# An FNet and SoLU kernel: block moves in runs of 256 bytes on two queues, one store for both batches, and a turn in five parts

## The chip, the cores and the metric

The kernel runs on one core of a Trainium2 chip. The metric is the device time of one execution in microseconds (us). Ratios are the mean time of one kernel's fast runs over that of the other's from the same rounds on the same chip, so they are not quite the ratio of the medians that stand beside them. The intervals are 95% intervals.

## The reference

```python
def _attn_ref(x):                        # x: 8 x 3136 x 256
    X = np.fft.fft(x, axis=1)
    X = np.fft.fft(X, axis=2)
    return X.real.astype(np.float32)

def _moe_ref(x, w_in, w_out, g_ln):      # x: the above as 25088 x 256, d_ff = 1024
    h = x @ w_in
    h_max = np.max(h, axis=-1, keepdims=True)
    e = np.exp(h - h_max)
    sm = e / (np.sum(e, axis=-1, keepdims=True) + 1e-09)
    solu = h * sm
    mu = np.mean(solu, axis=-1, keepdims=True)
    var = np.mean((solu - mu) ** 2, axis=-1, keepdims=True)
    ln = (solu - mu) / np.sqrt(var + 1e-06) * g_ln
    return (ln @ w_out).astype(np.float32)
```

## The kernel before

The batches go in four pairs. The sequence transform of 3136 = 49 x 64 is done in two steps; a pair has 25 values of k1, and each (pair, k1) is a *unit* of work: up-projection `ps_h` (line L195), SoLU on VectorE and ScalarE, down-projection `ps_o` (L276), store. There are 100 units. Three things matter here.

First, the activations must be transposed between the two projections. VectorE transposes blocks of 32 x 32 into `v`, and 16 DMAs of 64 KB, "moves", carry blocks between partitions into `uT`, which is the stationary operand of the down-projection.

```python
    def turn_blocks(t, s):
        if s == 0:
            t.v = fpool.tile([P, 4, 32, KF, 2], FP32, tag="v", name="v32", bufs=2)
        u = t.u[s].rearrange("p (c q r) -> p c q r", q=4, r=32)
        for o in (s,) if len(t.signs) == 2 else (0, 1):
            nc.vector.transpose(out=t.v[:, :, :, :, o].rearrange("p q n c -> p c q n"), in_=u)

    def move_blocks(t):
        t.uT = fpool.tile([P, 4, 32, KF, 2], FP32, tag="uT", name="uT", bufs=3)
        for i in range(4):
            for q in range(4):
                a, b = slice(32 * i, 32 * i + 32), slice(32 * q, 32 * q + 32)
                nc.sync.dma_start(out=t.uT[b, i], in_=t.v[a, q])

    def down(t, s):
        uT = t.uT.rearrange("p i n c s -> p (i n) c s")
        # ... 8 matmuls: nc.tensor.matmul(ps, uT[:, :, c, s], Wo[:, c, :], ...)
```

The last two indices of `v` and `uT` are c (8) and s (2): a run is 32 x 8 x 2 floats = 2 KB, and neighbouring n lie 64 bytes apart. Second, the results of a unit are stored by two DMAs, one a batch, and the mirrored ones by an indirect DMA. Third, `turn` brings a pair's sequence transform back from HBM with the roles of its indices exchanged: 3.2 MB on the sync queue, just before the pair is needed.

The main loop of units, in which every engine's program has this order:

```python
        for i in range(len(units) + 2):            # cur = unit i, nxt = i + 1, old = i - 2
            even(cur, up(cur, 0)); odd = up(cur, 1)
            nxt.q = take2(transform2(pairs[nxt.p], nxt.k1))
            join(cur, odd); expo(cur)
            ahead_pe(ahd, cur.k1)                  # the next pair's transform, and its turn
            ps_o = [down(old, s) for s in old.signs]
            for s in cur.signs: product(cur, s)
            for s in cur.signs: square(cur, s); turn_blocks(cur, s)
            store(old, 0, ps_o[0])
            move_blocks(cur); stats(cur)
            # ... loads of the next pair
            store(old, 1, ps_o[1])
```

(The conditions at the ends of the loop are cut.)

## Time and profile before

| | before |
|---|---|
| median of 3 runs | 1442.1 us (1441.77 to 1443.86) |
| TensorE busy | 1239.2 us, 86% |
| VectorE busy | 1084.9 us, 75% |
| DMA share, all queues of part 3 added | 51% |
| TensorE waits for `uT` | 79.5 us |

A profile page reads as follows: a group's line has the busy time and mean duration of one instruction, and after the second bar the time its engine sat idle just before, with what ended it. The chain of waits follows the last instruction back to what released it. TensorE's records overlap, so the mean duration of one is no pace (its busy time counts an overlap once); paces are taken from the timeline. The lines that carry the argument stand in the prediction.

### The profile page before, as it was taken

How to read it: one execution, taken by the hardware profiler on the slowest of the kernel's cores; microseconds unless marked ns; L12 is line 12 of the kernel's file. 1: busy time of each engine (PE TensorE's matmuls, PEld its weight loads, DVE VectorE, ACT ScalarE, POOL GpSimd, SP SyncE). 2: the span in 40 equal slices, each digit the busy share in tenths (PEclk: the TensorE clock that was granted, in tenths of full speed). 3: DMA queues.
4: the chain of work that ended last, by engine and by line, in shares of the span. 5: the costliest groups of instructions: out<-in, count | busy, mean ns of one | idle time of the engine just before them, and what ended most of it. 6: DMA issues, size and time to landing. Idle time of an engine off the chain costs nothing.

```text
span 1438.1 us, 17170 instructions
## 1 busy us (share of the span) xinstructions
PE 1239.2 (86%) x4864; PEld 996.2 (69%) x4864; DVE 1084.9 (75%) x1481; ACT 611.9 (43%) x1149; POOL 482.8 (34%) x892
## 2 busy tenths in 40 slices
PE   1543799999959999989959999999978999999996
PEld 1312587777848778878848778777857777878876
DVE  2597888787866688887857688877857778888881
ACT  1100445454434355544534444545524445444442
POOL 3400344443312345434213344434313223333331
PEclk8666899999989999999989999999998999999998
DMA  9540455554474555555474545555474444444443
GB/s 251 185 84 0 125 149 148 146 152 130 127 163 109 142 137 154 150 154 131 122 164 111 149 125 158 144 148 137 120 171 112 114 104 113 112 110 114 114 113 82
DMA packets 128318, 189.66 MB, mean 132 GB/s; under 512 B 36726, under 2 KB 63102, under 8 KB 127968
## 3 DMA queue, kind: packets, MB, share of 16 engines
q1 hardware_dynamic: 113552, 157.61, 43.6%
q0 software_dynamic: 8704, 25.44, 5.7%
q10 hardware_dynamic: 5968, 5.52, 1.7%
q8 instruction: 40, 0.66, 0.2%
q14 instruction: 54, 0.44, 0.1%
HBM read 44.78 MB, written 38.80 MB: 58 GB/s over the span
## 4 chain that ended last, share of the span: by engine, by line
PE 53%; SPq 24%; DMA 9%; DVE 8%; issue 4%; ACT 1%; POOL 1%; POOLq 0%; DVEq 0%; ACTq 0%
PE ps_o L276 33%; SPq L270 21%; PE ps_h L195 15%; DMA g<-zd 3%; DMA uT<-v 3%; PE ps L149 2%; SPq L290 2%; PE ps L169 2%; DMA xa<-in_x_dram 2%; DVE ex L303 2%; DVE h L209 1%; DVE v L262 1%; DMA xb<-in_x_dram,idx 1%; DVE y L111 1%; DMA out_dram<-ot 1%
## 5 line engine op out<-in xcount | busy, mean ns | idle before, releaser
L276 PE MATMUL ps_o<-Wo,uT 128*128 128x256 f32 x3136 | 750.3, 399 | 92.8 <-DMA uT<-v 79.5
L276 PEld LDWEIGHTS ps_o<-Wo,uT 128*128 128x128 f32 x3136 | 717.0, 307 | 116.2 <-issue 95.2
L262 DVE STREAM_TRANSPOSE v<-u 128x1024 f32<-128x1024 f32 x200 | 369.7, 1921 | 0.1
L195 PE MATMUL ps_h<-Wi,q 128*128 128x512 f32 x800 | 361.7, 595 | 4.8 <-DVE ev L201 3.7
L228 DVE SCALAR_TENSOR_TENSOR u<-h,u 128x1024 f32<-128x1024 f32 x196 | 232.7, 1223 | 140.6 <-ACT u L220 119.1
L220 ACT ACTIVATE u<-h,neg 128x1024 f32<-128x1024 f32 x196 | 223.7, 1142 | 211.7 <-DVE neg L214 185.0
L237 ACT ACTIVATE h<-u,nmean 128x1024 f32<-128x1024 f32 x196 | 223.7, 1142 | 200.7 <-POOL nmean L230 147.2
L209 DVE CUSTOM_DVE_ANT_0 h<-ev,ps_h 128x1024 f32<-128x1024 f32 x196 | 231.7, 1219 | 65.8 <-PE ps_h L195 31.1
L285 POOL DMA_INDIRECT out_dram<-ot,idx x96 | 113.0, 1177 | 481.5 <-DMA out_dram<-ot 301.5
L195 PEld LDWEIGHTS ps_h<-Wi,q 128*128 128x128 f32 x800 | 152.6, 191 | 152.3 <-issue 147.4
L201 DVE SCALAR_TENSOR_TENSOR ev<-w_mid,q,ps_h 128x1024 f32<-128x1024 f32 x100 | 125.8, 1258 | 66.4 <-PE ps_h L195 64.3
L230 POOL TENSOR_SCALAR nmean<-usum 128x1 f32<-128x1 f32 x196 | 94.8, 492 | 229.0 <-DVE u L228 227.6
L177 ACT COPY q<-ps 128x257 f32<-128x257 f32 x100 | 37.3, 373 | 233.0 <-PE ps L171 227.2
L149 PE MATMUL ps<-y,F 98*100 98x258 f32 (+3 forms) x288 | 79.4, 415 | 46.8 <-DVE y L111 46.8
L282 ACT ACTIVATE ot<-ps_o,rs 128x256 f32<-128x256 f32 x196 | 82.2, 457 | 53.7 <-PE ps_o L276 53.6
L169 PEld LDWEIGHTS ps<-T,g 128*128 128x128 f32 x400 | 60.4, 191 | 47.5 <-issue 47.4
L149 PEld LDWEIGHTS ps<-y,F 98*100 98x100 f32 x288 | 47.2, 187 | 59.9 <-issue 28.2
L249 POOL TENSOR_SCALAR v<-ssq 128x2 f32<-128x2 f32 (+1 forms) x100 | 24.6, 246 | 170.8 <-ACT h L237 170.8
L118 POOL TENSOR_TENSOR xa<-xa,xb 98x1020 f32<-98x1020 f32 (+1 forms) x32 | 72.7, 2273 | 27.4 <-DMA xa<-in_x_dram 18.8
L252 POOL TENSOR_TENSOR rs<-v,neg_half 128x2 f32<-128x2 f32 (+1 forms) x100 | 71.9, 719 | 7.8
L169 PE MATMUL ps<-T,g 128*128 128x128 f32 x400 | 60.7, 274 | 0.0
L109 DVE TENSOR_TENSOR y<-xa 98x508 f32<-98x508 f32 x32 | 21.4, 669 | 39.1 <-POOL xa L118 34.8
(52 smaller groups left out, 474.8 us busy)
## 6 DMA issues: line engine op xcount, KB each, us to landing
uT<-v SPq DMA_DIRECT2D x1600, 64.0 KB
zd<-z SPq DMA_DIRECT2D x32, 400.0 KB
g<-zd SPq DMA_DIRECT2D x16, 800.0 KB
out_dram<-ot SPq DMA_DIRECT2D x200, 64.0 KB
xa<-in_x_dram SPq DMA_DIRECT2D x32, 392.0 KB
raw_in_moe_w_in_dram<-in_moe_w_in_dram ACTq DMA_DIRECT2D x1, 2048.0 KB
raw_in_moe_w_out_dram<-in_moe_w_out_dram ACTq DMA_DIRECT2D x1, 2048.0 KB
out_dram<-ot,idx POOLq DMA_INDIRECT x96, 3.0
```

Of the source, the lines that this page charges most:

```text
L149: nc.tensor.matmul(o[..., cs], F[:, 2 * t + h, :], i[..., cs], start=first, stop=True, skip_group_check=True)
L169: nc.tensor.matmul(ps[:, h * P : (h + 1) * P], pr.g[:, k1, h * P : (h + 1) * P], T[:, k1, :], start=(h == 0), stop=True, skip_group_check= ...
L195: nc.tensor.matmul(ps[:, fs], t.q[:, c * P : (c + 1) * P], Wi[:, c, fs], start=True, stop=True)
L201: nc.vector.scalar_tensor_tensor(out=t.ev, in0=w_mid, scalar=t.q[:, KD * P :], in1=ps, op0=ALU.mult, op1=ALU.add)
L209: nc.vector.tensor_tensor_reduce(out=t.h[s], in0=t.ev, in1=ps, scale=1.0, scalar=-3.0e38, op0=ALU.subtract if s else ALU.add, op1=ALU.max, ...
L220: nc.scalar.activation(out=t.u[s], in_=t.h[s], func=ACT.Exp, bias=t.neg[:, s : s + 1], accum_out=t.esum[:, s : s + 1])
L228: nc.vector.scalar_tensor_tensor(out=t.u[s], in0=t.h[s], scalar=1.0, in1=t.u[s], op0=ALU.mult, op1=ALU.mult, accum_out=t.usum[:, s : s + 1])
L237: nc.scalar.activation(out=t.h[s], in_=t.u[s], func=ACT.Square, bias=t.nmean[:, s : s + 1], accum_out=t.ssq[:, s : s + 1])
L262: nc.vector.transpose(out=t.v[:, :, :, :, o].rearrange("p q n c -> p c q n"), in_=u)
L270: nc.sync.dma_start(out=t.uT[b, i], in_=t.v[a, q])
L276: nc.tensor.matmul(ps, uT[:, :, c, s], Wo[:, c, :], start=(c == 0), stop=(c == KF - 1))
L285: nc.gpsimd.indirect_dma_start(out=out, out_offset=bass.IndirectOffsetOnAxis(ap=idx[:, i : i + 1], axis=0), in_=ot, in_offset=None)
```

## The change

Its intent: elements of `v` and `uT` that an engine walks through lie 8 bytes apart and not 64, so that transposes and weight loads run faster; the price is that each row of a move falls into 8 runs of 256 bytes. A quarter of the moves goes to ScalarE's queue to relieve the sync queue, one store does for two, and the turn is cut into five parts on GpSimd's queue.

```diff
-        pr.g = gpool.tile([P, NK, D], FP32, tag="g", name="g")
+        pr.g[i] = gpool.tile([P, KG, D], FP32, tag="g", name="g")     # KG = 5, five parts, 6 buffers
         for j in range(4):
-            nc.sync.dma_start(out=pr.g[j * NH : (j + 1) * NH, :, :], ...)
+            k = j * NK + i * KG
+            nc.gpsimd.dma_start(out=pr.g[i][j * NH : (j + 1) * NH, :, :], ...)
...
-            t.v = fpool.tile([P, 4, 32, KF, 2], FP32, tag="v", name="v32", bufs=2)
+            t.v = fpool.tile([P, FF, 2], FP32, tag="v", name="v32", bufs=2)
+            t.uT = fpool.tile([P, KF, 4, 64], FP32, tag="uT", name="uT", bufs=3)
+        nc.vector.transpose(out=t.v[:, :, s], in_=t.u[s])
...
+    def move_blocks(t, engine, groups):
+        v = t.v.rearrange("p (c q n) s -> p q c (n s)", q=4, n=32)
+        for i in groups:
             for q in range(4):
-                nc.sync.dma_start(out=t.uT[b, i], in_=t.v[a, q])
+                engine.dma_start(out=t.uT[b, :, i, :], in_=v[a, q])
...
-        for b in range(2):
-            nc.sync.dma_start(out=ob[t.k1], in_=ot[b * N2 : (b + 1) * N2, :])
+        nc.sync.dma_start(out=out_k[t.p, t.k1], in_=ot)
...
-                move_blocks(cur)
+                move_blocks(cur, nc.sync, range(3))
+                move_blocks(cur, nc.scalar, (3,))
```

(Cut where marked, and inside lines with `...`.)

More of the change, by code (lines that the diff above doesn't have):

```diff
@@ L25 @@
 NC = NH // CH
+KG = 5
 EVEN, ODD = slice(0, 129), slice(129, 256)
@@ L61 @@
     x_pn = x.rearrange("b (n1 n2) d -> (b n1) n2 d", n2=N2)
-    out_b = out.rearrange("(b s) d -> b s d", b=B)
+    out_k = out.rearrange("(p k2 k1) d -> p k1 k2 d", p=NP, k1=N1)
     const = ctx.enter_context(tc.tile_pool(name="const", bufs=1))
@@ L66 @@
     zpool = ctx.enter_context(tc.tile_pool(name="zpool", bufs=2))
-    gpool = ctx.enter_context(tc.tile_pool(name="gpool", bufs=2))
+    gpool = ctx.enter_context(tc.tile_pool(name="gpool", bufs=6))
     qpool = ctx.enter_context(tc.tile_pool(name="qpool", bufs=3))
@@ L88, in __init__ @@
             self.raw, self.y, self.y0 = {}, {}, None
-            self.g = None
+            self.g = {}
     def load(pr, c):
@@ L154, in transform1, with turn @@
             nc.sync.dma_start(out=pr.zd[:, c * CH : (c + 1) * CH, :], in_=pr.z)
-    def turn(pr):
-        pr.g = gpool.tile([P, NK, D], FP32, tag="g", name="g")
+    def turn(pr, i):
+        pr.g[i] = gpool.tile([P, KG, D], FP32, tag="g", name="g")
         for j in range(4):
-            nc.sync.dma_start(out=pr.g[j * NH : (j + 1) * NH, :, :],
-                              in_=pr.zd[j * NK : (j + 1) * NK, :, :].rearrange("k n d -> n k d"))
+            k = j * NK + i * KG
+            nc.gpsimd.dma_start(out=pr.g[i][j * NH : (j + 1) * NH, :, :],
+                                in_=pr.zd[k : k + KG, :, :].rearrange("k n d -> n k d"))
     def transform2(pr, k1):
+        i, k = divmod(k1, KG)
+        g = pr.g[i]
         ps = ps_m.tile([P, KD * P + 1], FP32, tag="m", name="ps2")
         for h in range(KD):
-            nc.tensor.matmul(ps[:, h * P : (h + 1) * P], pr.g[:, k1, h * P : (h + 1) * P], T[:, k1, :],
+            nc.tensor.matmul(ps[:, h * P : (h + 1) * P], g[:, k, h * P : (h + 1) * P], T[:, k1, :],
                              start=(h == 0), stop=True, skip_group_check=True)
-        nc.tensor.matmul(ps[:, KD * P :], T[:, k1, :], pr.g[:, k1, P : P + 1],
+        nc.tensor.matmul(ps[:, KD * P :], T[:, k1, :], g[:, k, P : P + 1],
                          start=False, stop=True, skip_group_check=True)
@@ L258, in turn_blocks @@
         if s == 0:
-            t.v = fpool.tile([P, 4, 32, KF, 2], FP32, tag="v", name="v32", bufs=2)
-        u = t.u[s].rearrange("p (c q r) -> p c q r", q=4, r=32)
-        for o in (s,) if len(t.signs) == 2 else (0, 1):
-            nc.vector.transpose(out=t.v[:, :, :, :, o].rearrange("p q n c -> p c q n"), in_=u)
-    def move_blocks(t):
-        t.uT = fpool.tile([P, 4, 32, KF, 2], FP32, tag="uT", name="uT", bufs=3)
-        for i in range(4):
+            t.v = fpool.tile([P, FF, 2], FP32, tag="v", name="v32", bufs=2)
+            t.uT = fpool.tile([P, KF, 4, 64], FP32, tag="uT", name="uT", bufs=3)
+        nc.vector.transpose(out=t.v[:, :, s], in_=t.u[s])
+        if len(t.signs) == 1:
+            nc.vector.transpose(out=t.v[:, :, 1], in_=t.u[s])
+    def move_blocks(t, engine, groups):
+        v = t.v.rearrange("p (c q n) s -> p q c (n s)", q=4, n=32)
+        for i in groups:
             for q in range(4):
                 a, b = slice(32 * i, 32 * i + 32), slice(32 * q, 32 * q + 32)
-                nc.sync.dma_start(out=t.uT[b, i], in_=t.v[a, q])
+                engine.dma_start(out=t.uT[b, :, i, :], in_=v[a, q])
     def down(t, s):
-        uT = t.uT.rearrange("p i n c s -> p (i n) c s")
+        uT = t.uT.rearrange("p c i (n s) -> p c (i n) s", s=2)
         ps = ps_m.tile([P, D], FP32, tag="m", name="ps_o")
         for c in range(KF):
-            nc.tensor.matmul(ps, uT[:, :, c, s], Wo[:, c, :], start=(c == 0), stop=(c == KF - 1))
+            nc.tensor.matmul(ps, uT[:, c, :, s], Wo[:, c, :], start=(c == 0), stop=(c == KF - 1))
         return ps
@@ L287, in store @@
             return
-        for b in range(2):
-            ob = out_b[2 * t.p + b].rearrange("(k2 k1) d -> k1 k2 d", k1=N1)
-            nc.sync.dma_start(out=ob[t.k1], in_=ot[b * N2 : (b + 1) * N2, :])
+        nc.sync.dma_start(out=out_k[t.p, t.k1], in_=ot)
     def load_weight(pool, w, o, engine):
@@ L400, in ahead_pe @@
             transform1(pr, step - 4)
-        elif step - 4 == NH // 2:
-            turn(pr)
+        elif step - 4 >= NH // 2:
+            turn(pr, step - 4 - NH // 2)
     with tc.manual_schedule():
```

## The prediction

> **What bounds the kernel now.** I first read the page's chain of waits and its costliest groups, then the timeline of the sync queue and of TensorE in a steady stretch, then a pair boundary, and last the DMA view of two short windows, because the page's DMA share is a mean over very different stages. The chain names two owners: TensorE with 53% and the sync queue (SPq) with 24%.
>
> ```profile
> PE 53%; SPq 24%; DMA 9%; DVE 8%; issue 4%; ACT 1%; POOL 1%; POOLq 0%; DVEq 0%; ACTq 0%
> L276 PE MATMUL ps_o<-Wo,uT 128*128 128x256 f32 x3136 | 750.3, 399 | 92.8 <-DMA uT<-v 79.5
> L276 PEld LDWEIGHTS ps_o<-Wo,uT 128*128 128x128 f32 x3136 | 717.0, 307 | 116.2 <-issue 95.2
> L262 DVE STREAM_TRANSPOSE v<-u 128x1024 f32<-128x1024 f32 x200 | 369.7, 1921 | 0.1
> L195 PE MATMUL ps_h<-Wi,q 128*128 128x512 f32 x800 | 361.7, 595 | 4.8 <-DVE ev L201 3.7
> L195 PEld LDWEIGHTS ps_h<-Wi,q 128*128 128x128 f32 x800 | 152.6, 191 | 152.3 <-issue 147.4
> ```
>
> See that the same 128x128 fp32 weight load lasts 307 ns when it reads uT (columns 64 bytes apart) and 191 ns when it reads q (contiguous), and that a 128x1024 transpose takes 1921 ns, while other 128x1024 VectorE rows take 1219 to 1258 ns. The mean of 399 ns for a ps_o matmul is no pace, since records overlap. The pace is in the timelines:
>
> ```profile
> 1189.83 7.17 PEld L276 LDWEIGHTS ps_o<-Wo,uT 128*128 128x128 f32 x32 [0.42 <-PE ps L171]
> 1189.86 7.43 PE L276 MATMUL ps_o<-Wo,uT 128*128 128x256 f32 x32 [0.36 <-DMA uT<-v]
> 1189.89 10.04 SPq L270 DMA_DIRECT2D uT<-v  x16
> 1200.04 1.17 SPq L290 DMA_DIRECT2D out_dram<-ot  x2
> ```
>
> One unit (one k1 of one pair; 100 of them) gives TensorE 32 records of ps_o (7.10 us in some stretches of the chain, 7.43 in others), 8 of ps_h (3.43) and 0.57 for ps, 11.1 to 11.4 us. It gives the sync queue 16 moves and 2 stores, 10.04 + 1.17 = 11.2 us before any load. VectorE, too, is a full loop: 1.25 + 2.44 + 0.25 + 1.44 (it waits for the exponential) + 2.3 + 3.7 for two transposes = 11.4 us. So three bounds lie within 0.3 us of one another, and each hiccup of one is paid. The largest hiccup is the turn at a pair boundary:
>
> ```profile
> 399.40 4.32 SPq L160 DMA_DIRECT2D g<-zd  x4
> 403.84 4.29 SPq L290 DMA_DIRECT2D out_dram<-ot  x2
> 408.24 15.88 SPq L270 DMA_DIRECT2D uT<-v  x16
> 424.23 1.17 SPq L290 DMA_DIRECT2D out_dram<-ot  x2
> ...
> 425.65 2.90 PE L276 MATMUL ps_o<-Wo,uT 128*128 128x256 f32 x6 [13.27 <-DMA uT<-v]
> ```
>
> The 3.2 MB turn stands in the same queue ahead of the block moves; TensorE sits 13.27 us until they land. This happens at each of three boundaries. For the cost of short runs the kernel already holds a sample: table T is loaded in runs of 256 bytes (64 fp32). Two DMA windows:
>
> ```profile
> DMA packets 1110, 0.35 MB, mean 174 GB/s; under 512 B 1073, under 2 KB 1073, under 8 KB 1110
> ...
> DMA packets 8298, 11.23 MB, mean 112 GB/s; under 512 B 2560, under 2 KB 3712, under 8 KB 8290
> q1 hardware_dynamic: 7883, 9.99, 40.9%
> ```
>
> The first two lines are of different windows. 22 to 24 us is the end of T, with the DMA digits at 9: 1110 packets in 2 us on 16 engines are 16 x 2000 / 1110 = 29 ns a packet and engine; 16.5 to 18 us gave 716 in 1.5 us, 34 ns. 1200 to 1300 us is steady state without a pair being prepared: DMA is busy under half, so today it bounds nothing except at boundaries.
>
> **What the Trainium skill says.** "SBUF — State Buffer", section "Door 1: The DMA port swizzle", in its note on lines, speaks of 16-byte lines, of which at least two accesses must fall on one for full rate, so that 4-byte elements spaced wider than that pay. The trace agrees in direction: 307 against 191 ns, 1921 against some 1220 ns. The new spacing is 8 bytes, two to a line, so by that page free; no row of this kernel shows a weight load at 8 bytes, but VectorE reads raw weights at 8 bytes in 422 ns where contiguous ones take 428. "DMA: Bandwidth & Descriptors", section "Specifications", asks for at least 512 bytes a transfer for line rate, and its section "Why small descriptors are slow (HBM only)" says that copies within SBUF do not suffer this. T comes from HBM, so the trace can't decide between these; I take T's 29 to 34 ns as it stands. The same page, "Issuing engines are not separate DMA queues", says that all queues end on the same 16 engines and that a second queue saves only issue time: that is how I count the ScalarE part.
>
> **The change, part by part.**
> (1) Weight loads at 8 bytes. If 307 falls to about 191 ns, loads hide behind the stream of 256 columns. A 512-column record takes 3.43/8 = 0.429 us, so 256 columns take 0.2145, and 32 of them 6.86 us in place of 7.10 to 7.43. TensorE's unit: 6.86 + 3.43 + 0.57 = 10.86 us, and while a pair is prepared 16 transforms of 0.86 in 25 units add 0.55: 11.41.
> (2) Transposes at 8 bytes: 1921 to about 1220 ns, 2 x 0.7 = 1.4 us off VectorE's loop, 11.4 to 10.0, under TensorE.
> (3) Sync queue: 12 moves x 0.63 + 1 store x 0.6 = 8.2 us for 11.2. Four moves go to ScalarE, whose issues in the prologue take 0.4 to 0.7 us: about 2.2 us onto an engine that is busy 49 of the 100 us from 1200 on, 5.7 a unit. They stand after the squares, when the transposes are done, so I expect no wait in front of the next exponential.
> (4) DMA. Each move of 64 KB becomes 256 packets in place of 32; a unit has 16 x 256 = 4096 in place of 512. At 29 to 34 ns that is 4096 x 31.5 / 16 = 8.1 us, in place of about 4 us (16 bursts, seen as about 0.25 us each). The rest: 1200 to 1300 held 135 moves, 34 of the 44.6 us; 10.6 us over 8.5 units is 1.3 a unit. The share is 0.55 rather than 0.45 while a pair is prepared, 0.10 x 12 = 1.2 more. So DMA needs 9.4 us a unit in the last pair and 10.6 in the first three, 85 to 95% of TensorE's pace. It becomes a near-bound.
> (5) The turn in five parts on GpSimd's queue: each part is 640 KB, some 3 us at the 209 GB/s of the turn in the prologue, started up to four units before it is needed and interleaved with the moves. It takes away the three boundary stalls, 13 to 16 us each, some 45 us. GpSimd pays 20 issues of about 1.1 us (its indirect ones take 1177 ns) in five units of each pair, which may delay the means (nmean) by a few us each; small.
>
> **Sum.** The body starts at 137 us as before (the prologue waits for the weights' conversion, not for the turn). TensorE's floor is 75 x 11.41 + 25 x 10.86 = 1127, less 4 half units of 3.43 = 1113. The fill (two units without a down projection) and the tail cost some 30 us as now. 137 + 1113 + 30 = 1280. Against this floor the kernel before loses about 150 us; the near-full DMA queue will keep some loss: I allow 0.5 us a unit, 50 us, for moves that land late. About 1328 us.
>
> **Rivals.** (a) DMA becomes the bound: 256-byte packets within SBUF cost 45 ns, not 31.5 (each read and write also touches only 32 partitions). Then 11.5 + 2.5 = 14.0 and 12.8 us a unit: 170 + 75 x 14.0 + 25 x 12.8 = about 1540, slower. For it: the packet count grows eightfold, and HBM 1 KB packets take about 80 ns now. Against: T's measured 29 to 34 ns, of which even the HBM side is part. At 38 ns it would be about 1390 to 1420, hardly a gain. (b) Packets cheaper than T's, about 20 ns, as SBUF to SBUF: DMA hides and the time is near the floor, 1285 to 1300. (c) ScalarE is held by its DMA issues when the queue is full, as in the prologue, where its issue of T took 13.89 us for two; each us there moves the exponential, and VectorE's slack is only about 1 us. This would make 1370 to 1420. (d) The weight load is not the pace: ps_o stays at 7.1 to 7.4 us, 25 to 50 us are lost from the gain, about 1360.
>
> **Range and chances.** All parts but the DMA point down, and DMA has a sample in the trace with under 10% room on it. I say 1328 us, 1280 to 1430 for 8 in 10. Faster by over 2% (under 1413) 0.80, the same 0.10, slower 0.10, nearly all of that being rival (a).
>
> **What would show it.** Weight loads of ps_o near 191 ns and 32 records in 6.9 us; transposes near 1220 ns; no stall over 5 us at the boundaries; DMA digits 8 to 9 in the first three quarters; sync queue idle between units. Wrong would be: DMA digits of 9 throughout with TensorE waiting on uT<-v in every unit (a), ScalarE issues of over 1 us ahead of the exponential (c), or weight loads that stay near 300 ns (d).

## The result, and the profile after

The changed kernel took 1535.2 us (1530.37 to 1543.41, 4 runs) beside 1442.98 for the kernel before: ratio 1.064 (1.059 to 1.070). It is slower. The predicted time was 1328 us.

The page of the changed kernel, in the order of the views of before: the line of DMA packets, the chain of part 4 and the groups of part 5.

```profile
DMA packets 477182, 189.65 MB, mean 123 GB/s; under 512 B 445751, under 2 KB 459327, under 8 KB 476833
...
PE 36%; DMA 21%; DVE 15%; SPq 9%; ACT 7%; issue 7%; POOL 4%; ACTq 0%; POOLq 0%; DVEq 0%
...
L280 PE MATMUL ps_o<-Wo,uT 128*128 128x256 f32 x3136 | 780.8, 412 | 163.4 <-DMA uT<-v 75.9
L280 PEld LDWEIGHTS ps_o<-Wo,uT 128*128 128x128 f32 x3136 | 663.2, 214 | 262.4 <-issue 109.0
...
L264 DVE STREAM_TRANSPOSE v<-u 128x1024 f32<-128x1024 f32 x196 | 233.2, 1228 | 0.1
```

The two things the layout was made for came: the weight load fell from 307 to 214 ns in the mean (its median is 196) and the transpose from 1921 to 1228 ns. But TensorE's share of the chain fell from 53 to 36%, and DMA, VectorE, ScalarE and GpSimd all gained a share. A chain that runs through every engine is a latency loop: nothing is busy all the time, and each waits for the one before it. TensorE sat idle 163.4 us before `ps_o` instead of 92.8.

The waits of the sync queue, longest first (total us, times, longest). Before, the same view has 0.5 us in one wait for `uT<-v`:

```profile
SPq L274 <- DMA uT<-v: 403.2, 120, 7.4
```

The sync queue stands 403 us in front of a move until an *earlier move has landed*. It need not wait for data there, so this must be bookkeeping. The timeline of a steady stretch shows which. First the sync queue (start, length, queue, line, DMAs):

```profile
1299.49 8.65 SPq L274 DMA_DIRECT2D uT<-v  x9
1308.25 0.53 SPq L292 DMA_DIRECT2D out_dram<-ot  x1
1308.89 14.87 SPq L274 DMA_DIRECT2D uT<-v  x12
1323.87 0.53 SPq L292 DMA_DIRECT2D out_dram<-ot  x1
```

Twelve moves should take 12 x 0.65 = 7.8 us, and take 14.87. Then the chain of waits in the same stretch:

```profile
1316.19 1.14 POOL nmean L235
...
1317.35 0.25 ACT h L242
...
1318.41 1.15 ACT h L242 x2
1319.55 2.15 DMA uT<-v
...
1321.72 0.59 SPq L274
...
1322.35 2.29 DMA uT<-v
1324.64 0.96 issue
```

Sync has issued nine of its twelve by 1314.7 and then stands still. At 1319.55 ScalarE, having finished its squares, issues a move; 2.15 us later it has landed, and only now, from 1321.72 to 1323.76, sync issues the last three moves of *its* twelve. TensorE starts at 1325.60. But the twelve sync moves begun at 1308.89 belong to the unit before the one whose transposes and squares end at 1319.5. The data of unit n wait for a move of unit n+1.

```profile
1311.13 7.16 PE L280 MATMUL ps_o<-Wo,uT 128*128 128x256 f32 x32
1325.60 4.74 PE L280 MATMUL ps_o<-Wo,uT 128*128 128x256 f32 x13 [3.31 <-DMA uT<-v]
```

These are TensorE's two down-projections of that stretch (the second cut by the view's edge): TensorE stood idle for 3.31 us before the second. The whole second one lasts 8.84 us in the chain, not 7.0 to 7.2; the granted clock was 0.81 from 1325.6 to 1334.4 and 1.00 from 1311.1 to 1318.2. It goes on like this to 1470: each of the six down-projections that began after an idle spell of over 3 us lasted 8.84 us, and each of the six between them 7.16. That the idle spell is the cause is not shown.

**Where the wait comes from.** The built program (what the framework makes of the kernel) says it. DMAs that sync and ScalarE issue signal their landing on eight completion counters, shared by the two queues and handed out in turn; before a DMA may use a counter, its issuer waits for the DMA that had it before. Here is the order in which the counters are handed out, for one unit n (a listing of the built program, not of a run):

```
place  issued by  move of unit   waits for                    signals
 1222  sync       n              counter 4 >= 2144            counter 4
 1223  ScalarE    n+1            counter 5 >= 2144, VectorE   counter 5 -> 2160
 1224  sync       n              counter 6 >= 2144            counter 6
 ...
 1231  sync       n              counter 5 >= 2160            counter 5
```

At place 1231 sync waits, for a move of unit n, until ScalarE's move of unit n+1 from place 1223 has landed, and that one waits for the transposes of n+1. In the whole changed program 167 sync moves wait for a ScalarE move of the next unit. In the main loop of the kernel before only the sync queue uses these counters (ScalarE issues DMAs in the prologue alone), and its waits point backwards only.

DMA itself was not full. Its share in the last pair (1300 to 1480 us) was 30.9% + 9.0% in the two queues of the moves and 3.0% in GpSimd's.

### The profile page after: what moved, and what is told of

Read it like the earlier page. It is cut to its first block, busy times and chain, and to the rows that moved or that the text cites. A ratio compares the mean times of both kernels' runs of the same rounds, so it can differ in the third digit from the quotient of the medians.

```text
span 1536.9 us, 17200 instructions
## 1 busy us (share of the span) xinstructions
PE 1270.6 (83%) x4864; PEld 950.5 (62%) x4864; DVE 963.0 (63%) x1481; ACT 621.1 (40%) x1149; POOL 519.2 (34%) x972
## 4 chain that ended last, share of the span: by engine, by line
PE 36%; DMA 21%; DVE 15%; SPq 9%; ACT 7%; issue 7%; POOL 4%; ACTq 0%; POOLq 0%; DVEq 0%
PE ps_o L280 25%; DMA uT<-v 14%; PE ps_h L200 10%; SPq L274 8%; DVE h L214 6%; ACT h L242 4%; DMA out_dram<-ot 4%; ACT u L225 3%; DVE u L233 2%; POOL nmean L235 2%; DMA xa<-in_x_dram 2%; DVE ex L305 2%; POOL out_dram L289 1%; DMA zd<-z 1%; DVE v L264 1%
## 5 line engine op out<-in xcount | busy, mean ns | idle before, releaser
L280 PE MATMUL ps_o<-Wo,uT 128*128 128x256 f32 x3136 | 780.8, 412 | 163.4 <-DMA uT<-v 75.9
L280 PEld LDWEIGHTS ps_o<-Wo,uT 128*128 128x128 f32 x3136 | 663.2, 214 | 262.4 <-issue 109.0
L233 DVE SCALAR_TENSOR_TENSOR u<-h,u 128x1024 f32<-128x1024 f32 x196 | 232.5, 1223 | 140.0 <-ACT u L225 123.3
L264 DVE STREAM_TRANSPOSE v<-u 128x1024 f32<-128x1024 f32 x196 | 233.2, 1228 | 0.1
L286 ACT ACTIVATE ot<-ps_o,rs 128x256 f32<-128x256 f32 x196 | 91.2, 465 | 236.2 <-DMA uT<-v 165.4
L235 POOL TENSOR_SCALAR nmean<-usum 128x1 f32<-128x1 f32 x196 | 82.4, 432 | 170.1 <-DVE u L233 166.3
L163 POOL DMA_DIRECT2D g<-zd x80 | 47.7, 607 | 9.7 <-DMA zd<-z 8.5
```

What stands on the lines that cost most here:

```text
L233: nc.vector.scalar_tensor_tensor(out=t.u[s], in0=t.h[s], scalar=1.0, in1=t.u[s], op0=ALU.mult, op1=ALU.mult, accum_out=t.usum[:, s : s + 1])
L264: nc.vector.transpose(out=t.v[:, :, s], in_=t.u[s])
L280: nc.tensor.matmul(ps, uT[:, c, :, s], Wo[:, c, :], start=(c == 0), stop=(c == KF - 1))
```

## The experiments

Theory: this coupling through counters costs the time. Rival 1: packets of 256 bytes are slow in the DMA engines (rival (a) of the prediction). Rival 2: ScalarE is held up by issuing (rival (c)). Every run below gave a correct result. In the texts "waits of sync" is the total of the sync queue's waits for `uT<-v` before a move.

### e1: everything on sync again

```diff
-                move_blocks(cur, nc.sync, range(3))
-                move_blocks(cur, nc.scalar, (3,))
+                move_blocks(cur, nc.sync, range(4))
```

> The changed kernel with all 16 block moves of a unit on the sync queue again (nothing on ScalarE); runs of 256 bytes, one store and the turn in five parts stay. Theory (counter coupling): DMAs of sync and ScalarE share eight completion counters, handed out in an order in which ScalarE's moves of unit n+1 stand before the last sync moves of unit n; so sync waits for moves that are issued only after the next unit's transposes. With one queue this cannot be: about 1340 us (sync needs 16 x 0.64 + 0.55 = 10.8 us a unit, TensorE 10.9 to 11.4), waits of the sync queue for uT<-v under 60 us (403 in the changed kernel). Rival 1 (packets of 256 bytes are slow in the DMA engines): nothing is taken away, at least 1500 us. Rival 2 (ScalarE is held up by its own DMA issues): also faster than 1535, 1340 to 1400, so this run doesn't separate it from the theory.

Measured: 1383.09 us (1381.73 to 1388.49), ratio to before 0.957 (0.954 to 0.961).

```profile
SPq L274 <- DMA uT<-v: 9.3, 18, 1.4
```

This is the sync queue's line of waits in e1: 403.2 us became 9.3. Putting a quarter of the moves on a second queue had cost 152 us. The absolute time is 43 us above what I expected; e8 explains that. Rival 1 is out as the main cause, for all packets of 256 bytes are still there. They are even cheap. The DMA view of the last pair, of e1 (1180 to 1340 us) and of the kernel before (1205 to 1400 us), each with its packets, MB and share of 16 engines:

```profile
q1 hardware_dynamic: 62818, 16.43, 46.6%
```

```profile
q1 hardware_dynamic: 15424, 19.68, 41.2%
```

In e1 that is 0.466 x 160 x 16 / 62818 = 0.019 us, 19 ns a packet in the mean, stores and counters included. In the time of DMA per unit (223 moves are 13.9 units, 267 are 16.7): 0.466 x 160 / 13.9 = 5.4 us, and 0.412 x 195 / 16.7 = 4.8 us before. Eight times the packets cost 0.6 us of DMA time a unit and not the 4 that I had added.

### e2: half of the moves on ScalarE

```diff
-                move_blocks(cur, nc.sync, range(3))
-                move_blocks(cur, nc.scalar, (3,))
+                move_blocks(cur, nc.sync, range(2))
+                move_blocks(cur, nc.scalar, (2, 3))
```

> The changed kernel with 8 moves of a unit on sync and 8 on ScalarE (not 12 and 4). In the built program of this split no sync move waits for a ScalarE move of a later unit (167 do in the changed kernel). Theory (counter coupling): clearly faster than 1535, 1340 to 1420 us, with waits of sync for uT<-v under 100 us, although ScalarE issues twice as many DMAs. Rival 2 (ScalarE held up by its issues): slower than 1535, 1560 or more, as 8 x 0.62 = 5 us of issue stand in its unit instead of 2.5. Rival 1 (slow packets): at least 1500.

Measured: 1389.19 us (1387.12 to 1392.06), ratio 0.962 (0.958 to 0.965). Waits of sync were 67.6 us. Twice as many issues on ScalarE made the kernel 146 us *faster*, so rival 2 is out as the main cause. It is not wrong altogether: the chain of e2 has ScalarE's queue at 13%, where the changed kernel has 0%, so with 8 moves ScalarE's issuing has come onto the chain itself.

### e3 and e11: the runs of 256 bytes alone, and with the one store

e3 is the kernel before with the new `v`, `uT`, moves and `down`, all on sync; e11 has the one store in addition.

```diff
-            t.v = fpool.tile([P, 4, 32, KF, 2], FP32, tag="v", name="v32", bufs=2)
+            t.v = fpool.tile([P, FF, 2], FP32, tag="v", name="v32", bufs=2)
...
 # e11 only:
-        for b in range(2):
-            nc.sync.dma_start(out=ob[t.k1], in_=ot[b * N2 : (b + 1) * N2, :])
+        nc.sync.dma_start(out=out_k[t.p, t.k1], in_=ot)
```

> The kernel before with the runs of 256 bytes alone (transposes, moves and weight loads at 8 bytes; all on sync; two stores; turn in one on sync). Theory: packets of 256 bytes are not the trouble, weight loads and transposes get faster, the three boundary stalls stay: 1380 to 1410 us. Rival 1 (slow packets): 1500 or more.

Measured: 1485.83 us (1483.48 to 1491.92), ratio 1.028 (1.025 to 1.032). This is a miss: the layout that makes transposes and weight loads faster makes the whole slower by 43 us. The sync timeline of e3:

```profile
1207.32 10.46 SPq L269 DMA_DIRECT2D uT<-v  x16
1217.90 1.18 SPq L289 DMA_DIRECT2D out_dram<-ot  x2
```

Sixteen moves take 10.46 us to issue, where the kernel before took 10.04: 0.654 against 0.628 us a move. Over 1600 moves these 0.026 us are 42 us. The chain of e3 has the sync queue at 41% (24% before): VectorE and TensorE were made faster, but sync set the pace. I took that explanation to a test:

> The kernel before with runs of 256 bytes and the one store, all on sync, turn in one. Theory (the runs alone cost 43 us in e3 because each move takes 0.026 us more of the sync queue, which bounds): sync has 16 x 0.654 + 0.53 + gaps = 11.1 to 11.2 us a unit, 0.65 less than in e3: 1415 to 1430 us. If instead the packets' time in the DMA engines made e3 slow, the store takes away no 256-byte packet: over 1460.

Measured: 1419.8 us (1419.77 to 1420.12), ratio 0.984 (0.980 to 0.988), as expected: an issue of about 0.65 us less a unit gives 66 us (64 by the ratios), although no packet of 256 bytes was taken away.

### e4 and e8: the old runs of 2 KB under the rest of the change

e4 is the changed kernel with the old layout, still 12 moves on sync and 4 on ScalarE; e8 has the old layout and all moves on sync.

```diff
-            t.v = fpool.tile([P, FF, 2], FP32, tag="v", name="v32", bufs=2)
-            t.uT = fpool.tile([P, KF, 4, 64], FP32, tag="uT", name="uT", bufs=3)
+            t.v = fpool.tile([P, 4, 32, KF, 2], FP32, tag="v", name="v32", bufs=2)
+            t.uT = fpool.tile([P, 4, 32, KF, 2], FP32, tag="uT", name="uT", bufs=3)
...
```

(The transposes, the moves and `down` follow the layout; e8 has e1's edit in addition.)

> The changed kernel with the old layout of v and uT (runs of 2 KB, 64-byte spacing), all else as changed, 12 moves on sync and 4 on ScalarE. Here the build happens to order the counters so that sync waits only for ScalarE moves of its own unit (398 waits, none for a later unit). Theory: no loop through the next unit, so faster than 1442, VectorE's loop of 11.4 us and the missing boundary stalls give 1370 to 1400. Rival 1 (slow packets): the same, 1370 to 1400, since the packets are large again; so this run alone does not separate the two, it tells what the split costs without the coupling. Rival 2 (ScalarE held by issues): stays over 1480.

Measured: 1337.39 us (1335.02 to 1341.4), ratio 0.926 (0.922 to 0.930), better than expected. Waits of sync are 26.7 us. The same split of 12 and 4 is harmless where the built program couples only within one unit. It doesn't tell the theory from rival 1 by itself, as said beforehand. TensorE is now the bound: it spent 11.30 us a unit, start to start, without a gap.

> The kernel before with one store for both batches and the turn in five parts on GpSimd alone: runs of 2 KB as before, all moves on sync. Sync needs 10.05 + 0.35 = 10.4 us a unit for 11.2 and the boundary stalls go; VectorE's loop of 11.4 us then bounds. Theory: 1340 to 1375 us. With e1 (the same with runs of 256 bytes, 1383) it tells what the short runs cost where sync is near its limit: 16 x 0.026 us more issue a unit, some 40 us or less.

Measured: 1342.65 us (1339.63 to 1344.58), ratio 0.928 (0.925 to 0.931). Against e8, e1 has only the short runs in addition and is slower by 0.957 - 0.928 = 0.029 of 1443 us, 42 us: the same sum as in e3. This is what I had missed in the expectation for e1. Set beside e4 these two runs do speak against rival 1: the short runs cost 42 us with all moves on sync, but 198 us under the split of 12 and 4 (e4 to the changed kernel), and of the two programs with that split only the changed kernel's has waits for a later unit.

### e5: only two moves on ScalarE

```diff
+SCALAR = ((3, 2), (3, 3))
...
-                engine.dma_start(out=t.uT[b, :, i, :], in_=v[a, q])
+                engine = nc.scalar if (i, q) in SCALAR else nc.sync
+                engine.dma_start(out=t.uT[b, :, i, :], in_=v[a, q])
...
```

> The changed kernel with 14 moves of a unit on sync and only 2 on ScalarE. In the built program 167 sync moves still wait for a ScalarE move of the following unit, as many as in the changed kernel with its 4. Theory (counter coupling): still slow, 1480 to 1550 us, and waits of sync for uT<-v over 300 us, although half as much is issued on ScalarE. Rival 2 (ScalarE held up by its issues) and plain load sharing: between the all-sync run (1383) and less, 1350 to 1385.

Measured: 1538.1 us (1531.54 to 1541.57), ratio 1.065 (1.062 to 1.068): as slow as the changed kernel with half of ScalarE's issues.

```profile
SPq L276 <- DMA uT<-v: 279.9, 114, 6.1
```

Waits of sync are 280 us, a little under the 300 that I had named.

### e6: ScalarE's moves one unit later in its program

```diff
                 expo(cur)
+            if prev:                              # prev = unit i - 1
+                move_blocks(prev, nc.scalar, (3,))
...
-                move_blocks(cur, nc.scalar, (3,))
```

> The changed kernel, 12 moves on sync and 4 on ScalarE as there, but ScalarE's 4 of a unit are put into its program one unit later, after the next unit's exponential. In the built program 1 sync move waits for a ScalarE move of a following unit (167 in the changed kernel), 387 for one of its own unit. Theory (counter coupling): most of the loss goes, 1300 to 1350 us, sync's waits for uT<-v under 150 us. Rival 2 (ScalarE held up by issues): no better than 1535, as these issues now stand inside the chain from exponential to squares.

Measured: 1474.39 us (1472.27 to 1477.79), ratio 1.020 (1.017 to 1.023). A miss: of the loss, only 61 us went. Waits of sync are still 361.3 us:

```profile
SPq L274 <- DMA uT<-v: 361.3, 100, 7.9
```

In the built program they are now, all but one, for ScalarE moves of sync's own unit. The chain of e6 shows why:

```profile
1178.12 0.14 ACT u L225
...
1178.30 2.87 DMA uT<-v
...
1181.19 0.59 SPq L274
```

ScalarE issues the move after the next unit's exponential, it lands at 1181.17, and eight sync moves of 0.61 us, 5.2 us with the gaps, still follow before TensorE gets its data at 1188.6. So the harm is not that the counter belongs to a later *unit*. It is that sync stands behind a DMA that another engine issues late in its own program, with much left to do behind it. Both placings did that. The count of waits for a later unit was too narrow a sign.

### e7: the quarter on GpSimd's queue

```diff
-                move_blocks(cur, nc.scalar, (3,))
+                move_blocks(cur, nc.gpsimd, (3,))
```

> The changed kernel with the 4 ScalarE moves of a unit on GpSimd's queue, which has counters of its own; no sync move waits for a move of a later unit. Theory: sync is relieved (12 x 0.65 + 0.55 = 8.4 us a unit) and nothing is coupled, so TensorE bounds at 11.0 to 11.5 us a unit: 1300 to 1340 us. If GpSimd is held up by its DMA issues (some 0.6 to 1.2 us each, 4 a unit) so that the means come late, 1340 to 1400.

Measured: 1316.65 us (1312.06 to 1322.36), ratio 0.910 (0.906 to 0.913). This is the fastest of all, 9% under the kernel before and 14% under the changed one. GpSimd's DMAs have counters of their own, and the built program has no sync move that waits for one of a later unit. In a steady stretch TensorE runs without gaps:

```profile
1152.53 7.16 PE L280 MATMUL ps_o<-Wo,uT 128*128 128x256 f32 x32
1159.52 3.60 PE L200 MATMUL ps_h<-Wi,q 128*128 128x512 f32 x8
1162.96 0.61 PE L174 MATMUL ps<-T,g 128*128 128x128 f32 x4
1163.40 0.28 PE L176 MATMUL ps<-g,T 128*128 128x1 f32 x2
1163.54 7.16 PE L280 MATMUL ps_o<-Wo,uT 128*128 128x256 f32 x32
```

A unit is 1163.54 - 1152.53 = 11.01 us, against 11.30 in e4: here at last the faster weight loads pay.

### e9: six moves on ScalarE

The edit is that of e5, with the last six (i, q) in `SCALAR`.

> The changed kernel with 10 moves of a unit on sync and 6 on ScalarE. In the built program no sync move waits for a ScalarE move of a later unit (167 do with 4 on ScalarE, 167 with 2), 282 wait for one of their own unit. Theory (a sync move that waits for a ScalarE move issued after the next unit's transposes): fast, 1310 to 1360 us, sync's waits for uT<-v under 150 us, although ScalarE issues half as many again as in the changed kernel. Rival 2 (ScalarE held up by its issues): slower than 1535. If only the count of ScalarE moves mattered, time would rise 2, 4, 6 on ScalarE: 1538, 1535, more.

Measured: 1326.71 us (1321.4 to 1332.87), ratio 0.920 (0.915 to 0.925). Waits of sync are 99.8 us before a move, but those before its stores and the next pair's DMAs bring all its waits for `uT<-v` to 210.2 us, which is over the 150 that I had named:

```profile
SPq L276 <- DMA uT<-v: 99.8, 70, 4.3
...
SPq L294 <- DMA uT<-v: 55.2, 15, 5.3
SPq L99 <- DMA uT<-v: 37.3, 15, 3.1
...
SPq L157 <- DMA uT<-v: 17.9, 6, 4.7
```

With 2, 4, 6 and 8 moves on ScalarE the times are 1538, 1535, 1327 and 1389 us, while the waits for a later unit in the built programs are 167, 167, 0 and 0. The number of moves on ScalarE does not order the times; the two slow splits are the two with waits for a later unit. The total of sync's waits does not order them either: e9 has more of it than e2 (67.6 us) and is faster, and e5 has less than the changed kernel and is as slow. What a wait costs hangs on what is left to do behind it; that reading comes from the chains, e6's above all, and no run tested it by itself.

### e10: the one store alone

The edit is e11's second part, on the kernel before.

> The kernel before with the one store for both batches alone. Sync's issue falls from 10.05 + 1.17 to 10.05 + 0.5 us a unit, VectorE's loop of 11.4 us and TensorE's 11.3 then bound; the boundary stalls stay. Theory: 1385 to 1405 us; the rest down to e8 (1343), 45 us or so, is the turn in five parts.

Measured: 1385.19 us (1384.11 to 1385.86), ratio 0.960 (0.956 to 0.964).

## Why the prediction was wrong

With the ratios, each times 1443 us, the change comes apart like this (the three jobs ran on different chips, each beside its own runs of the kernel before; by the intervals each step is uncertain by 6 to 9 us):

| step | ratio from, to | us |
|---|---|---|
| one store (before to e10) | 1 to 0.960 | -58 |
| turn in five parts (e10 to e8) | 0.960 to 0.928 | -46 |
| runs of 256 bytes (e8 to e1) | 0.928 to 0.957 | +42 |
| four moves to ScalarE (e1 to the changed kernel) | 0.957 to 1.064 | +154 |
| sum | 1 to 1.064 | +92 |

The step that failed is (3), the sync queue. It counted issues only, "12 moves x 0.63 + 1 store x 0.6 = 8.2 us for 11.2", and said of ScalarE's four "I expect no wait in front of the next exponential". I asked whether the moves would hold up ScalarE, and not whether ScalarE's moves would hold up sync. The sum was right for the issues (0.609 us in the median) but 403 us of waits came on top, and sync, forecast to be idle between units, stood still inside them; by the table the four moves cost 154 us. The waits for counters stand in the built program, which can be listed without a run; the prediction did not ask which DMA each counter had last belonged to. None of the signs of being wrong that it named was this one. With the quarter off sync but on counters of its own (e7) the time was 1317 us, so the rest of the sum (1328) was about right in total, though it had allowed 50 us for a near-full DMA queue that did not come.

The others, in the prediction's order. (1) Weight loads: right in kind (196 ns in the median); 32 records took 7.00 us in e7 and not 6.86. (2) Transposes: 1228 ns for the predicted 1220. (4) DMA: wrong in size and in the safe direction, 0.6 us more a unit instead of about 4; the DMA digits of the changed kernel's page lie between 4 and 7 in the first three quarters after the prologue, not at 8 to 9. My sample was table T's load from HBM with 29 to 34 ns a packet, and moves within SBUF came to 19 ns. The Trainium skill had said that copies within SBUF do not suffer from small descriptors ("DMA: Bandwidth & Descriptors", section "Why small descriptors are slow (HBM only)"), and I set T's number above it, though T was another kind of transfer. (5) The turn: predicted some 45 us, measured 46; from e10 to e8 TensorE's waits for `uT<-v` and `out_dram<-ot` before `ps_o` fell from 55.8 to 22.8 us and the longest from 13.1 to 4.7, so 33 of the 46 us are seen as stalls that went. GpSimd's issues of it took 607 ns each, not 1.1 us. Three sums slip without weight in this: 1280 + 50 is 1330, not 1328; the kernel before lies 162 us above the floor of 1280, not 150; and rival (a)'s formula gives 1363 us at 38 ns a packet, not 1390 to 1420.

Rival (a) named about 1540 us, and 1535 came. It was right by accident: it wanted the DMA engines full and packets of 45 ns, and they were busy 43% of the last pair, with 19 ns a packet in e1. Had I stopped at the number, the explanation would have been wrong.

What I also had not seen is that the sum's parts were not additive. As long as sync set the pace, faster transposes and weight loads were worth nothing, and 0.026 us more per issue was worth 42 us (e3). Only where sync was relieved without waits for a later unit did the short runs gain: e7 (1317 us) and, less clearly, e9 (1327), against 1337 in e4.

Open: why the framework hands the counters out in that order for 2 and 4 moves and not for 6 and 8. I did not try an order of its own with the split and the placing of the changed kernel kept. Between the profiled executions of e1 and of the changed kernel, 150 us apart, TensorE's busy time for the same matmuls rose by 51 us (1219.6 to 1270.6, mean clock 0.945 and 0.907) and its idle time by 99. So about a third of the loss is slower matmuls; whether the idle spells cause the lower clock stays open.

## What to carry to other kernels

Before you spread DMAs over a second queue, find out what the two queues share besides the DMA engines: if they share completion counters, one queue can stand behind a DMA that another engine issues late in its own program. In the profile it shows as a queue that waits for the landing of a transfer it doesn't need, with DMA far from full and a chain that goes through all engines. And a saving on engines that didn't set the pace was worth nothing here (e3), while 4% on the issue of each DMA counted in full on the queue that did.

## What the Trainium skill lacked or had wrong

- "DMA: Bandwidth & Descriptors", "Issuing engines are not separate DMA queues", says that a second queue saves only sequencer time. It can also cost: moving 4 of 16 moves to ScalarE's queue took the kernel from 1383 to 1535 us, with DMA busy 43% in the last pair. No page that I read says that completion counters shared by two issuers can stall one behind the other.
- The same section calls the time to issue a DMA usually small beside the DMA. Here 16 issues of 0.628 us were a bound of the kernel. The page gives no figure for how issue time grows with the runs of a row: 0.628 us with one run of 2 KB, 0.654 with eight of 256 bytes (10.04 and 10.46 us for 16), worth 42 us.
- Its section "Why small descriptors are slow (HBM only)" was right for moves within SBUF: 19 ns a packet on average in e1, against the 29 to 34 ns of T's load from HBM. Falling below the 512 bytes of its section "Specifications" cost little here: 5.4 us of DMA time a unit in place of 4.8.
- "SBUF — State Buffer", "Door 1: The DMA port swizzle", its note on lines of 16 bytes, held: at 8 bytes in place of 64 the weight load took 196 ns for 307 and the transpose 1228 for 1921. It lacks what this is worth for a stream of matmuls: the down-projection's 32 records took 7.00 us (e7) in place of 7.28 (e4), from their start to that of the next group.
